# Sink attention and a soft mixture of experts on one core: the cast of q and k between the exponentials, in the rounds around a sequence's first block

## The chip, the cores and the metric

The kernel runs on one core of a Trainium2 chip, as one program. The metric is the time of one execution on the device in microseconds; lower is better. The core's engines are TensorE (PE in the profile, its weight loads PEld), VectorE (DVE), ScalarE (ACT), GpSimd (POOL) and SyncE (SP), which here only issues transfers. Each works through its own list of instructions in order and waits on semaphores for the others.

## The reference: what is computed

Attention over 4 sequences of 768 tokens with 8 heads of 64, where a token sees the first 4 tokens (the sinks) and the last 128; then a mixture of 8 experts whose weights come from 8 rounds of normalising rows and columns. Cut to what matters:

```python
scores = scale * np.matmul(q, k.transpose(0, 1, 3, 2))
keep = is_sink | in_window            # first 4 keys, or the last 128
scores = np.where(keep, scores, -1000000000.0)
a = np.exp(scores - np.max(scores, axis=-1, keepdims=True))
a = a / (np.sum(a, axis=-1, keepdims=True) + 1e-09)
attn = np.matmul(a, v)                # 4 x 8 x 768 x 64
x = attn.transpose(0, 2, 1, 3).reshape(3072, 512)
P = np.exp(x @ w_gate - max)          # 3072 x 8, then 8 rounds of P /= row sums, P /= column sums
for e in range(8):
    out += P[:, e:e + 1] * (np.maximum(x @ w1[e], 0.0) @ w2[e])
```

All is fp32. The kernel multiplies fp32 numbers as two parts, a rounded high part and the low part that is left; most operands are split by a cast on ScalarE (high) and a subtraction on VectorE (low), and a product is three matmuls.

## The kernel before, in words

The attention comes first and takes some 290 us; the matmuls of the experts fill the rest and, a few at a time, the gaps of the attention. The tokens are worked in 48 units: unit n is (sequence b, block i of 128 tokens, half hh of four heads), so a sequence has 12 units and its first block (i = 0) is units 0 and 1, 12 and 13, 24 and 25, 36 and 37. A token block attends to itself and the block before it; the first block has nothing before it and no separate sinks, so for its units TensorE has three matmuls with V for two heads, where others have six and one with the sinks.

The units run as a software pipeline. Round n (`steady_round`, from n = 10 on) does the scores, the maxima and the exponentials of unit n + 1, transposes q and k of unit n + 2, transposes the probabilities of unit n and multiplies those of unit n - 1 with V. Within a round the engines' orders are written out by hand: what the code calls first stands first on its engine, and no scheduler changes it. The steps, with the lines of the profile:

- `scores` (L484): TensorE, 12 matmuls of 128x260 for four heads, each head into a PSUM bank of its own, st0 to st3. There is one buffer of each, so a bank must have been read before it is written again.
- `soften` (L492, L495): for each head VectorE adds the mask and takes the row's extreme (L492), then ScalarE takes the exponential with its row sum (L495). The four heads go one after the other.
- `values` for the first pair of heads (L558) and six matmuls of an expert's first layer (`run_fill`, L660) on TensorE. Every second time these complete a sum, ScalarE applies the relu (L665) and VectorE makes its low part (L666), which waits in the list `late`.
- `transpose_qk` (L446, L450, L453, L456): TensorE transposes q and k of the unit after the next into st0, ScalarE casts the high part into the tile `KQ` (L450), and a function that it returns has VectorE subtract the low part (L453) and, where i = 1, copy the sink columns (L456). That function is put into the list `lows`. The next round's scores read the result.
- `divide` (L501, L502, L504): VectorE adds 1e-9 to the four row sums and inverts them, GpSimd scales the probabilities of the four heads. L501 needs the sums of all four exponentials.
- `late`, then `lows`: the relu's low part, then that of q and k.
- `transpose_p` twice (L515, L517, L520): TensorE transposes the probabilities of two heads into st1, then of the other two into st2; ScalarE casts the high part PT (L517), VectorE subtracts the low part (L520). In a first block these tiles are 256 wide, else 512.
- `values` for the second pair, `store_x` (L568, copies of the result on ScalarE and VectorE), the transposed sinks (L538, L540), and a second portion of expert matmuls (L676).

GpSimd's list in a round is the gathered sinks (L532, L533), the split of V (L464, L465) and the scaling (L504); in the rounds of a first block also the sinks of the new sequence spread over the heads (L419) and split (L425, L426), and in some rounds the low part of the finished tokens (L577).

So ScalarE's order in a round is: four exponentials, the relu if there is one, the cast of q and k, two casts of probabilities, the copy of the result. VectorE's is: four extremes, the row sums and their inverse, the relu's low part, the low part of q and k, two low parts of probabilities, the copy. The code that sets it:

```python
        if on(n + 1):
            for h in range(HH):
                soften(n + 1, (h,))
...
        lows = [transpose_qk(n + 2)] if on(n + 2) else []
        flush(mid)
        behind[0] = True
        if on(n + 1):
            divide(n + 1, range(HH))
        flush(late)
        flush(lows)
```

Of the kernel before, what the change touches and what calls it, by code (L numbers as in the profile page):

```python
# [229 lines left out]
def tile_sink_attention_moe(ctx: ExitStack, tc: tile.TileContext, q, k, v, wg, w1, w2, out):  # L230
# [17 lines left out]
    HH = H // 2  # L248
# [59 lines left out]
    def split_gate():  # L308
        for kc in range(KC):
            nc.vector.tensor_copy(wgr[:, kc, :], zero)  # L310
        nc.vector.tensor_copy(wgr[:, :, 0:E], wg_raw)
        nc.vector.tensor_sub(wgr[:, :, E:2 * E], wg_raw, f32(wgr[:, :, 0:E]))
        nc.vector.tensor_add(sel, ident[0:2 * E, 0:E], ident[0:2 * E, E:2 * E])
# [82 lines left out]
    units = [(b, i, hh) for b in range(B) for i in range(NB) for hh in range(2)]  # L396
    us = {}
# [8 lines left out]
    def flush(todo):  # L406
        for f in todo[:]:
            f()
        todo.clear()

    def load_sinks(b):
        vs = VSr[b] = att.tile([SK, D], F32, name="vs")
        for r0 in range(0, SK, NK):
            (nc.sync if b else nc.scalar).dma_start(vs[r0:r0 + NK, :], v[b, :, 0:SINK, :])
# [13 lines left out]
    def load_rows(names, j):  # L428
        b, i = divmod(j, NB)
        cuts = (0, HH, H) if j == 0 else (0, H)  # L430
        ts = [(att.tile([P, H, D], F32, name=nm), {"kr": k, "qr": q, "vr": v}[nm]) for nm in names]
        for (t, _), nm in zip(ts, names):
            raws[nm, b, i] = t
        for h0, h1 in zip(cuts, cuts[1:]):
            for t, src in ts:
                nc.sync.dma_start(t[:, h0:h1, :], src[b, h0:h1, i * P:(i + 1) * P, :].rearrange("h p d -> p h d"))
# [47 lines left out]
                nc.tensor.matmul(ps[h], lhsT=Q[r0:r0 + D, a, pr, :], rhs=K[r0:r0 + D, c, pr, :],  # L484
                                 start=(j == 0), stop=(j == 2))

    def soften(n, hs):

        b, i, hh = units[n]
        sc, st, ps = (us[n][x] for x in ("sc", "st", "ps"))  # L490
        for h in hs:
            nc.vector.tensor_tensor_reduce(out=sc[:, h, :], in0=ps[h], in1=masks[place(b, i).start, min(i, 2)], op0=ALU.add, op1=ALU.min,  # L492
                                           scale=-scale, scalar=3.0e38, accum_out=st[:, 0, h:h + 1])
        for h in hs:
            nc.scalar.activation(sc[:, h, :], sc[:, h, :], AF.Exp, bias=st[:, 0, h:h + 1], scale=-1.0, accum_out=st[:, 1, h:h + 1])  # L495

# [116 lines left out]
    def gate_step():  # L613
        if gates and next(gates[0], 0) == 0:
            gates.pop(0)
            gate_step()
# [104 lines left out]
    def run_fill(k_):  # L721
        for _ in range(k_):
            next(fill, None)
# [43 lines left out]
    on = lambda j: 0 <= j < L  # L767

    def early_round(n):

        if units[n + 2][2] == 0:
            with (tc.high_priority() if n == -2 else nullcontext()):
                load_rows(("kr", "qr"), n // 2 + 1)
                load_rows(("vr",), n // 2 + 1)
            if units[n + 2][1] == 0:
                load_sinks(units[n + 2][0])
        if n == -2:
            nc.sync.dma_start(wg_raw, wg.rearrange("(k p) e -> p k e", p=P))
        if n == 2:
            with tc.issue_after(us[1]["split"][1]):  # L780
                split_gate()
        if on(n + 1):
            for pr in range(NP):
                scores(n + 1, pr)
                soften(n + 1, range(2 * pr, 2 * pr + 2))
                divide(n + 1, range(2 * pr, 2 * pr + 2))
        if on(n - 1):
            values(n - 1, 0)
        if n >= START:
            run_fill(1)  # L790
        gate_step()
        for j in (0, 1) if n == -2 else (n + 2,) if n >= 0 else ():
            transpose_qk(j)()
        if on(n):
            transpose_p(n, 0)()
            with (tc.issue_after(us[n - 1]["scaled"]) if n > 1 else nullcontext()):
                split_v(n)
        gate_step()
        if on(n):
            transpose_p(n, 1)()  # L800
        if on(n - 1):
            values(n - 1, 1)
            store_x(n - 1)
        gate_step()
        if on(n) and units[n][1]:
            gather_sinks(n)
            transpose_sinks(n)
        if on(n) and units[n][1:] == (0, 1):
            with tc.issue_after(us[n]["scaled"]):
                spread_sinks(units[n][0])  # L810
                split_sinks(units[n][0])
        if n >= START:
            run_fill(1)
# [3 lines left out]

    def steady_round(n):

        if n % 2 == 0:  # L820
            if on(n + 2):
                load_rows(("vr",), n // 2 + 1)
            for j in (n // 2 + 1, n // 2 + 2) if n == STEADY else (n // 2 + 2,):
                if on(2 * j):
                    load_rows(("kr", "qr"), j)
            if on(n + 2) and units[n + 2][1] == 0:
                load_sinks(units[n + 2][0])
        if n in ROWS:
            ROWS[n][0](ROWS[n][1])
        mid.extend(coming)  # L830
        coming.clear()
        behind[0] = False
        if on(n + 1):
            for pr in range(NP):
                scores(n + 1, pr)
        if on(n):
            if units[n][1]:
                gather_sinks(n)
            split_v(n)
        if on(n + 1):  # L840
            for h in range(HH):
                soften(n + 1, (h,))
        if on(n - 1):
            values(n - 1, 0)
        run_fill(1)
        gate_step()
        lows = [transpose_qk(n + 2)] if on(n + 2) else []
        flush(mid)
        behind[0] = True
        if on(n + 1):  # L850
            divide(n + 1, range(HH))
        flush(late)
        flush(lows)
        if on(n):
            lows.append(transpose_p(n, 0))
        gate_step()
        if on(n):
            lows.append(transpose_p(n, 1))
        flush(lows)
        if on(n - 1):  # L860
            values(n - 1, 1)
            store_x(n - 1)
        gate_step()
        if on(n) and units[n][1]:
            transpose_sinks(n)
        run_fill(1)
        if n in PIECES:
            in_turn(*plain_tiles(*PIECES[n]))
        if n == L - 8:
            first_pieces.extend(pieces1(0))  # L870
        if n in (L - 8, L - 6, L - 4, L - 3):
            in_turn(*first_pieces.pop(0))
        flush(act_end)
        if on(n):
            b, i, hh = units[n]
            if (i, hh) == (0, 0):
                spread_sinks(b)
            elif (i, hh) == (0, 1):
                split_sinks(b)
        flush(pool_end)  # L880
        if L - 10 <= n < L - 6:
            sums1(0, n - (L - 10))
# [327 lines left out]
    hs = {}  # L1210
# [450 lines left out]
```

## Time and profile before

| what | value |
|---|---|
| time, median of 3 runs | 2137.17 us (2137.05 to 2137.85) |
| the profiled execution | 2136.98 us, of which the span from the first to the last instruction is 2135.3 us |
| TensorE busy | 2118.8 us, 99% of the span |
| VectorE, ScalarE, GpSimd busy | 1525.7, 883.9 and 749.6 us |
| granted TensorE clock | 1.000 throughout |
| rounds 12 to 14, 24 to 26, 36 to 38 start (first score matmul) | 82.18, 154.22 and 224.16 us |

A row of a timeline reads: start in us, duration in us, engine, line, operation, the tile written and those read, shapes, how many in a row, and in brackets how long the engine had been idle and which instruction ended that. A row of the list of waits reads: who waited for whom, us in total, how often, the longest. A duration goes to the end of the writing, so the next instruction of the same engine may start some 0.1 us before it.

### The profile page before, as it was taken

The numbers are of one execution on the slowest core, as the hardware profiler recorded it, in microseconds if no ns is written. First come the engines' busy times: TensorE is split into PE (matmuls) and PEld (weight loads), VectorE is DVE, ScalarE is ACT, GpSimd is POOL, SyncE is SP. The second block draws the span as 40 slices with busy tenths as digits, with TensorE's granted clock in tenths as the row PEclk, the third lists the DMA queues.
The fourth block names the chain that finished last, engine by engine and source line by source line (L and its number), as shares of the span: only waits on it lengthen the run. The fifth ranks groups of instructions, "written<-read, shape, count | busy, mean of one in ns | idle before, by whom it ended". The sixth has DMA issues, their size and how long they took to land.

```text
span 2135.3 us, 31724 instructions
## 1 busy us (share of the span) xinstructions
PE 2118.8 (99%) x10501; PEld 1770.3 (83%) x10501; DVE 1525.7 (71%) x2747; ACT 883.9 (41%) x1867; POOL 749.6 (35%) x950
## 2 busy tenths in 40 slices
PE   8999999999999999999999999999999999999998
PEld 7898897888888888888888888888888888888887
DVE  8777778877777876766666666666657666676666
ACT  7777745444444444442333223332333223332232
POOL 7756643333232331232223322233323222232223
PEclk9999999999999999999999999999999999999999
DMA  6534427999999987686666666667866666666662
GB/s 144 127 84 100 95 80 244 312 307 315 289 315 292 307 290 251 213 283 202 204 194 200 207 193 201 207 198 262 298 203 196 199 207 194 201 207 189 206 197 86
DMA packets 397641, 453.82 MB, mean 213 GB/s; under 512 B 99680, under 2 KB 265760, under 8 KB 396576
## 3 DMA queue, kind: packets, MB, share of 16 engines
q1 hardware_dynamic: 397080, 451.57, 68.0%
q8 instruction: 86, 1.41, 0.3%
q14 instruction: 83, 0.68, 0.1%
q10 hardware_dynamic: 392, 0.16, 0.0%
HBM read 314.17 MB, written 137.46 MB: 212 GB/s over the span
## 4 chain that ended last, share of the span: by engine, by line
PE 94%; DVE 3%; ACT 2%; issue 0%; POOL 0%; DMA 0%; SPq 0%; DVEq 0%; ACTq 0%; POOLq 0%
PE c L926 41%; PE o L1485 20%; PE held L1485 8%; PE held L1170 7%; PE o L1170 7%; PE O L558 3%; PE st L484 2%; PE st L515 1%; PE o L676 1%; PE g L660 1%; ACT sc L495 1%; PE st L446 1%; PE st L660 0%; DVE PT L520 0%; DVE KQ L453 0%; DVE sc L492 0%
## 5 line engine op out<-in xcount | busy, mean ns | idle before, releaser
L952 ACT CAST hf<-w 128x512 fp32r<-128x512 f32 x448 | 265.5, 622 | 562.3 <-POOL w L1452 299.8
L1485 PE MATMUL o<-hf,W2q 128*128 128x512 f32 x1920 | 472.0, 389 | 0.0
L1485 PEld LDWEIGHTS o<-hf,W2q 128*128 128x128 f32 x1920 | 360.0, 188 | 75.4 <-DVE acc L1499 0.9
L926 PE MATMUL c<-T,W1q 128*128 128x512 f32 x1530 | 388.8, 389 | 0.2 <-DVE w L1433 0.2
L953 DVE TENSOR_TENSOR hf<-w,hf 128x512 fp32r<-128x512 f32 x448 | 330.4, 765 | 74.8 <-ACT hf L952 67.0
L926 PEld LDWEIGHTS c<-T,W1q 128*128 128x128 f32 x1530 | 286.8, 188 | 60.7 <-DVE w L1433 0.9
L1499 DVE TENSOR_TENSOR acc<-o,acc 128x512 f32<-128x512 f32 x298 | 204.7, 687 | 171.2 <-PE o L1485 171.2
L926 PE MATMUL c<-B,W1q 128*128 128x512 f32 x1134 | 278.3, 389 | 0.0
L1452 POOL TENSOR_TENSOR w<-w 128x512 f32<-128x512 f32 x64 | 82.8, 1293 | 492.4 <-DVE w L1434 492.4
L926 PEld LDWEIGHTS c<-B,W1q 128*128 128x128 f32 x1134 | 212.6, 188 | 44.0
L1433 DVE TENSOR_TENSOR w<-c,M 128x512 f32<-128x512 f32 x192 | 132.2, 689 | 138.2 <-PE c L926 132.9
L1429 ACT COPY M<-c 128x512 f32<-128x512 f32 x192 | 112.7, 587 | 248.9 <-PE c L926 248.8
L1485 PE MATMUL held<-hf,W2q 128*128 128x512 f32 x768 | 194.8, 389 | 0.0
L926 PE MATMUL c<-T,W1f 128*128 128x512 f32 x672 | 171.1, 390 | 0.1
L1170 PE MATMUL held<-W2f,h 128*128 128x512 f32 x672 | 171.1, 390 | 0.0
L1170 PE MATMUL o<-W2f,h 128*128 128x512 f32 x672 | 170.6, 389 | 0.1
L1485 PEld LDWEIGHTS held<-hf,W2q 128*128 128x128 f32 x768 | 144.0, 188 | 29.8
L1467 POOL TENSOR_TENSOR w<-w 128x512 f32<-128x512 f32 x64 | 105.7, 1652 | 176.0 <-DVE hf L953 176.0
L1170 PEld LDWEIGHTS o<-W2f,h 128*128 128x128 f32 x672 | 126.0, 188 | 27.0 <-DVE acc L1177 0.9
L926 PEld LDWEIGHTS c<-T,W1f 128*128 128x128 f32 x672 | 125.8, 188 | 26.9 <-issue 0.5
L1170 PEld LDWEIGHTS held<-W2f,h 128*128 128x128 f32 x672 | 125.9, 188 | 26.4 <-DVE W2f L953 0.5
L979 POOL TENSOR_TENSOR r<-r 128x256 f32<-128x256 f32 x27 | 20.1, 743 | 359.3 <-ACT M L1133 222.9
(224 smaller groups left out, 3086.7 us busy)
## 6 DMA issues: line engine op xcount, KB each, us to landing
W2q<-w2s SPq DMA_DIRECT2D x448, 256.0 KB, 3.1
W1q<-w1s SPq DMA_DIRECT2D x444, 256.0 KB, 2.9
w1s<-W1f SPq DMA_DIRECT2D x56, 896.0 KB, 7.5
w2s<-WT SPq DMA_DIRECT2D x136, 256.0 KB, 3.6
r<-in_moe_w_dram SPq DMA_DIRECT2D x64, 512.0 KB, 4.6
w2s<-W2f SPq DMA_DIRECT2D x56, 256.0 KB, 4.8
PB<-psd SPq DMA_DIRECT2D x16, 512.0 KB, 3.8
w2s<-W2f SPq DMA_DIRECT2D x56, 128.0 KB, 6.5
```

Source lines behind the costliest of these rows:

```text
L484: nc.tensor.matmul(ps[h], lhsT=Q[r0:r0 + D, a, pr, :], rhs=K[r0:r0 + D, c, pr, :], start=(j == 0), stop=(j == 2))
L558: nc.tensor.matmul(u["O"][:, pr], lhsT=x_, rhs=y_, start=(j == 0), stop=(j == len(ops) - 1))
L926: nc.tensor.matmul(ps, lhsT=w1(a, k), rhs=x[:, b, k, :], start=(start and j == 0), stop=(stop and j == len(TERMS) - 1), skip_group_check=n ...
L952: nc.scalar.copy(dst[:, 0], src)
L953: at(1, lambda: nc.vector.tensor_sub(dst[:, 1], src, f32(dst[:, 0])))
L1170: nc.tensor.matmul(o, lhsT=h[c, th][:, a, off:off + P], rhs=W2F[n][:, w, c, :], start=(begin and c == 0 and j == 0), stop=(end and c == 1 ...
L1429: nc.scalar.copy(t, T["c2"])
L1433: nc.vector.tensor_add(w, T["c1"], T[m])
L1452: nc.gpsimd.tensor_sub(S3, T["A11"], T["A21"])
L1467: at(k, lambda: nc.gpsimd.tensor_sub(T["A11"], w, T["A11"]))
L1485: nc.tensor.matmul(o, lhsT=W2Q[part, n, m][:, a, k * P:(k + 1) * P], rhs=F[part, n, H_OF[m]][:, w, :], start=(j == 0 and (begin or not hol ...
L1499: nc.vector.tensor_add(sums[m, k], o, sums[m, k])
```

## The change

`soften` is cut in two, `maxima` (VectorE's part) and `exponentials` (ScalarE's). In a round of which unit n or unit n - 1 is of a first block (`short`; from the tenth round on these are rounds 12, 13, 14, 24, 25, 26, 36, 37 and 38) only two exponentials stand ahead of the transposes of q and k. The cast of q and k follows on ScalarE, its low part on VectorE is made at once, then the other two exponentials come, and the row sums after them. In all other rounds, and in the first ten, each engine's order is as before.

```diff
-    def soften(n, hs):
+    def maxima(n, hs):
...
+    def exponentials(n, hs):
+
+        sc, st = us[n]["sc"], us[n]["st"]
         for h in hs:
             nc.scalar.activation(sc[:, h, :], sc[:, h, :], AF.Exp, bias=st[:, 0, h:h + 1], scale=-1.0, accum_out=st[:, 1, h:h + 1])
...
     def steady_round(n):
 
+        short = on(n + 2) and 0 in (units[n][1], units[n - 1][1])
...
         if on(n + 1):
-            for h in range(HH):
-                soften(n + 1, (h,))
+            maxima(n + 1, range(HH))
+            exponentials(n + 1, range(2 if short else HH))
...
         lows = [transpose_qk(n + 2)] if on(n + 2) else []
         flush(mid)
         behind[0] = True
+        if short:
+            flush(lows)
+            exponentials(n + 1, range(2, HH))
         if on(n + 1):
             divide(n + 1, range(HH))
         flush(late)
         flush(lows)
```

From the exponential on, lines stand four further on in the changed kernel (the exponential is L499 there, the sums L505 and L506, the low part of the probabilities L524), and behind `steady_round` nine further on.

ScalarE in round 24, before. The names: sc the scores, h the expert's hidden tile, KQ the split q and k, st a PSUM bank, PT the probabilities, xr the result.

```order
L495 ACTIVATE sc,st<-sc,st 128x260 x4
L665 ACTIVATE h_2388<-g_2595 128x256
L450 CAST KQ_174<-st_2704 128x2x2x128
L517 CAST PT<-st_2720 128x256
L517 CAST PT<-st_2725 128x256
L568 COPY xr<-O 64x256
```

And in the changed kernel:

```order
L499 ACTIVATE sc,st<-sc,st 128x260 x2
L669 ACTIVATE h_2388<-g_2595 128x256
L450 CAST KQ_174<-st_2702 128x2x2x128
L499 ACTIVATE sc,st<-sc,st 128x260 x2
L521 CAST PT<-st_2720 128x256
L521 CAST PT<-st_2725 128x256
L572 COPY xr<-O 64x256
```

The third and fourth exponential have moved behind the relu and the cast of q and k.

VectorE in the same round, before, from the end of the extremes (L492) on. L589 is a gate column of the experts, copied out of PSUM.

```order
L492 ISA sc,st<-st_2670,mask_79 128x260
L492 ISA st 128x1
L589 COPY Xt<-O 128x8
L501 TENSOR_SCALAR st<-st 128x4
L502 RECIPROCAL st<-st 128x4
L666 SCALAR_TENSOR_TENSOR h_2388<-g_2595,h_2388 128x256
L453 TENSOR_TENSOR KQ_174<-st_2704,KQ_174 128x2x2x128
L456 CAST KQ_174<-KQ_174 128x4x4
L520 TENSOR_TENSOR PT<-st_2720,PT 128x256
L520 TENSOR_TENSOR PT<-st_2725,PT 128x256
```

And in the changed kernel:

```order
L492 ISA sc,st<-st_2670,mask_79 128x260
L492 ISA st 128x1
L593 COPY Xt<-O 128x8
L453 TENSOR_TENSOR KQ_174<-st_2702,KQ_174 128x2x2x128
L456 CAST KQ_174<-KQ_174 128x4x4
L505 TENSOR_SCALAR st<-st 128x4
L506 RECIPROCAL st<-st 128x4
L670 SCALAR_TENSOR_TENSOR h_2388<-g_2595,h_2388 128x256
L524 TENSOR_TENSOR PT<-st_2720,PT 128x256
L524 TENSOR_TENSOR PT<-st_2725,PT 128x256
```

The low part of q and k, with the sink columns, has moved ahead of the row sums; the low parts of the probabilities stay last. TensorE's, GpSimd's and SyncE's lists are the same.

More of the change, by code (lines that the diff above doesn't have):

```diff
@@ L784, in early_round @@
                 scores(n + 1, pr)
-                soften(n + 1, range(2 * pr, 2 * pr + 2))
+                maxima(n + 1, range(2 * pr, 2 * pr + 2))
+                exponentials(n + 1, range(2 * pr, 2 * pr + 2))
                 divide(n + 1, range(2 * pr, 2 * pr + 2))
```

## The prediction

> **What bounds the kernel now.** I read the page first, for the engine that sets the span.
>
> ```profile
> span 2135.3 us, 31724 instructions
> ...
> PE 2118.8 (99%) x10501; PEld 1770.3 (83%) x10501; DVE 1525.7 (71%) x2747; ACT 883.9 (41%) x1867; POOL 749.6 (35%) x950
> ```
>
> TensorE is busy for all but 16.5 us of 2135.3, and its order is fixed by hand, so whatever makes it wait in the attention part is carried to the end, and a wait taken away there is gained. The profiled execution took 2136.98 us, 1.7 more than its span and 0.19 less than the median of 2137.17; I work from 2136.98. Next I asked for TensorE's waits from 76 to 246 us, the stretch that holds all nine rounds that the change touches (12 to 14, 24 to 26, 36 to 38):
>
> ```profile
> PE st L484 <- DVE KQ L456: 1.0, 1, 1.0
> PE st L484 <- DVE PT L520: 0.6, 3, 0.2
> ```
>
> Only the scores (L484) wait, 1.6 us in all: once for the low part of k and q (L453, with the copy of the sink columns L456 behind it), three times for the low part of the probabilities (L520), whose PSUM banks the next round's scores overwrite. So two VectorE steps compete to end last. The change brings one forward, and the question is what it does to the other. The timeline of rounds 24 and 25 shows the chain. ScalarE:
>
> ```profile
> 156.97 0.50 ACT L495 ACTIVATE sc<-sc,st 128x260 f32<-128x260 f32 x1
> ...
> 157.46 0.36 ACT L665 ACTIVATE h<-g 128x256 fp32r<-128x256 f32 x1
> 157.72 0.57 ACT L450 CAST KQ<-st 128x512 fp32r<-128x512 f32 x1
> 158.19 0.37 ACT L517 CAST PT<-st 128x256 fp32r<-128x256 f32 x1
> ```
>
> The first row is the fourth exponential; the next ones start 0.5, 0.26 and 0.47 us after each other. VectorE, in the same round:
>
> ```profile
> 157.59 0.17 DVE L501 TENSOR_SCALAR st<-st 128x4 f32<-128x4 f32 x1 [0.29 <-ACT sc L495]
> 157.79 0.18 DVE L502 RECIPROCAL st<-st 128x4 f32<-128x4 f32 x1
> 157.88 0.40 DVE L666 SCALAR_TENSOR_TENSOR h<-g,h 128x256 fp32r<-128x256 f32 x1
> 158.33 0.69 DVE L453 TENSOR_TENSOR KQ<-st,KQ 128x512 fp32r<-128x512 f32 x1
> 158.93 0.18 DVE L456 CAST KQ<-KQ 128x16 fp32r<-128x16 f32 x1
> 159.02 0.74 DVE L520 TENSOR_TENSOR PT<-st,PT 128x256 fp32r<-128x256 f32 x2
> ```
>
> VectorE waits for the fourth exponential (L501 starts 0.62 after it), then works without a gap to L520. TensorE, rounds 24 to 26 (the first, third and fifth row are the last transpose of q and k of a round, the others the first product with V after the scores of the next):
>
> ```profile
> 157.30 0.27 PE L446 MATMUL st<-ident,qr 128*128 128x128 f32 x1
> ...
> 160.40 0.62 PE L558 MATMUL O<-PT,V 128*128 128x256 f32 x3
> ...
> 162.08 0.27 PE L446 MATMUL st<-ident,qr 128*128 128x128 f32 x1
> ...
> 165.38 0.62 PE L558 MATMUL O<-PT,V 128*128 128x256 f32 x3
> ...
> 167.04 0.27 PE L446 MATMUL st<-ident,qr 128*128 128x128 f32 x1
> ```
>
> ```profile
> 170.06 1.23 PE L484 MATMUL st<-KQ 64*128 64x260 f32 x11 [0.21 <-DVE PT L520]
> 171.22 0.98 PE L558 MATMUL O<-PT,V 128*128 128x256 f32 x6
> ```
>
> And VectorE's sums and low parts of rounds 25 and 26:
>
> ```profile
> 162.85 0.17 DVE L501 TENSOR_SCALAR st<-st 128x4 f32<-128x4 f32 x1 [1.12 <-ACT sc L495]
> ...
> 164.00 0.75 DVE L520 TENSOR_TENSOR PT<-st,PT 128x256 fp32r<-128x256 f32 x2
> ...
> 167.84 0.45 DVE L501 TENSOR_SCALAR st<-st 128x4 f32<-128x4 f32 x1 [0.81 <-ACT sc L495]
> ...
> 169.32 1.28 DVE L520 TENSOR_TENSOR PT<-st,PT 128x512 fp32r<-128x512 f32 x2
> ```
>
> TensorE's first product comes 1.38 us after L520 starts (159.02 to 160.40, 164.00 to 165.38), and 1.90 after it where the low parts are twice as wide (169.32 to 171.22). So the start of L520 is the clock that TensorE follows in these rounds.
>
> **The change part by part.** No instruction is added or removed; names and line numbers below are those of the kernel before.
>
> The exponentials. The cast L450 now stands between the second and the third, so these two wait until TensorE has transposed q and k. The transposes end 0.27 after their last start; I put the cast 0.04 behind that, as L453 starts 0.04 after the cast's end above (157.72 + 0.57 = 158.29, and 158.33). In round 24 the cast then starts at 157.30 + 0.27 + 0.04 = 157.61, which is only 0.11 before the 157.72 of now. The two exponentials that are left follow 0.47 later and 0.50 apart, and L501 0.62 behind the last: 157.30 + 1.90 = 159.20, where it is 157.59 now. So the sums come 1.61 later to buy 0.11 for the cast. The relu L665 stays ahead of the cast, and its matmuls ahead of the transposes, so it does not end last.
>
> The low part. L453 and L456 run in VectorE's wait, from 158.2 to 159.0. Behind L501 the path to L520 is then shorter: 0.20 and 0.09 to L666 and 0.30 more (0.40 less the 0.1 by which L520 overlaps L456), 0.60 in all with a relu's low part, 0.30 without. L520 starts at 159.20 + 0.60 = 159.80, **0.78 later** than the 159.02 of now. ScalarE's cast of the probabilities, 0.50 behind the fourth exponential, is out by 159.4 and hides.
>
> Round 25 starts 0.78 late. L501: 162.08 + 0.78 + 1.90 = 164.76; no relu here, so L520 at 165.06, **1.06 late** in all. Round 26: L501 at 167.04 + 1.06 + 1.90 = 170.00. Its length is 0.17 or 0.45 in the rows above; the long one ran until GpSimd's L464 was out (167.84 + 0.45 = 168.29 against 167.85 + 0.41):
>
> ```profile
> 163.41 1.87 POOL L504 TENSOR_SCALAR sc<-sc,st 128x260 f32<-128x260 f32 x4 [1.20 <-ACT KQ L450]
> ...
> 167.85 0.41 POOL L464 TENSOR_SCALAR V<-vr 128x256 fp32r<-128x256 f32 x1
> ```
>
> L504 follows L501 by 0.56, so it moves to 165.32, and L464, 4.44 behind it, ends at 170.17: L501 takes 0.19. Then 0.04 + 0.09 + 0.30 to L520 at 170.62, **1.30 late** (1.28 with 0.17, 1.56 with 0.45). The third sequence has the same rows 69.9 us later,
>
> ```profile
> 228.96 0.74 DVE L520 TENSOR_TENSOR PT<-st,PT 128x256 fp32r<-128x256 f32 x2
> ...
> 239.25 1.28 DVE L520 TENSOR_TENSOR PT<-st,PT 128x512 fp32r<-128x512 f32 x2
> ```
>
> so it costs 1.30 too. The first one, rounds 12 to 14, has the long wait for the low part. TensorE, VectorE and GpSimd:
>
> ```profile
> 85.09 0.27 PE L446 MATMUL st<-ident,qr 128*128 128x128 f32 x1
> ...
> 89.87 0.27 PE L446 MATMUL st<-ident,qr 128*128 128x128 f32 x1
> ...
> 92.63 1.21 PE L484 MATMUL st<-KQ 64*128 64x260 f32 x12 [0.99 <-DVE KQ L456]
> ...
> 95.28 0.27 PE L446 MATMUL st<-ident,qr 128*128 128x128 f32 x1
> ```
>
> ```profile
> 86.98 0.74 DVE L520 TENSOR_TENSOR PT<-st,PT 128x256 fp32r<-128x256 f32 x2
> ...
> 91.13 0.46 DVE L501 TENSOR_SCALAR st<-st 128x4 f32<-128x4 f32 x1 [1.43 <-ACT sc L495]
> ...
> 92.39 0.74 DVE L520 TENSOR_TENSOR PT<-st,PT 128x256 fp32r<-128x256 f32 x2
> ...
> 97.57 1.28 DVE L520 TENSOR_TENSOR PT<-st,PT 128x512 fp32r<-128x512 f32 x2
> ...
> 101.94 0.68 DVE L501 TENSOR_SCALAR st<-st 128x4 f32<-128x4 f32 x1 [1.12 <-ACT sc L495]
> ```
>
> ```profile
> 86.11 1.86 POOL L504 TENSOR_SCALAR sc<-sc,st 128x260 f32<-128x260 f32 x4 [2.34 <-DVE st L502]
> ...
> 90.83 0.74 POOL L465 TENSOR_TENSOR V<-vr,V 128x256 fp32r<-128x256 f32 x1
> ```
>
> Round 12: L501 at 85.09 + 1.90 = 86.99, L520 at 87.59, 0.61 late. Round 13: L501 at 89.87 + 0.61 + 1.90 = 92.38. GpSimd's L504 is at 86.99 + 0.56 = 87.55 and L465, 4.72 behind, runs 92.27 to 93.01, so L501 ends at 93.03 and L520 starts 0.13 later, at 93.16: 0.77 late, or 0.29 if L501 takes 0.17. Here the 0.99 of TensorE goes (the low part is done by 92.3), but L520 starts its wait anew. Round 14: L501 at 97.95, with 0.32 by the same reckoning of GpSimd's queue, L520 at 98.70, 1.13 late (0.50 with short L501s throughout). The next round's L501, 0.68 long now, finds GpSimd at another place and gives back some 0.1: 1.0 for this sequence, between 0.5 and 1.1.
>
> On this one step a rule bears. The Trainium skill, page "SBUF — State Buffer", section "SBUF: two separate sides", says that VectorE and GpSimd share a port pair that the first comer holds for its whole instruction while the other is blocked. The rows agree (0.17 alone, 0.45 until L464 is out); were the 0.46 of round 13 a fixed length instead, the first sequence would cost about 0.8 and the sum would be 3.4.
>
> The sum: 1.0 + 1.3 + 1.3 = **3.6 us**, from 3.1 (0.5 + 2 x 1.28) to 4.25 (1.13 + 2 x 1.56). 2136.98 + 3.6 = **2140.6**. The rounds behind have no recorded wait of TensorE that could take the delay in. SyncE's order and GpSimd's are unchanged, so loads and stores only shift with the buffers.
>
> **The rivals.** A measurement of this kernel can tell about 0.2%, 4.3 us, from no change: 2132.9 and 2141.4 are the bounds.
>
> Not slower: the low part of q and k decides, and L520 comes no later. For it speaks the largest wait, 1.0 for L456. It decides if the sums are delayed by less than VectorE's path to L520 is shortened; against it, in round 24 they are 1.61 against 0.84 (159.02 less 157.88 + 0.30), in round 25 1.13 of its own against 0.85, and for the balance to turn the transposes would have to end half a microsecond sooner. It would save at most the 1.6 of the waits: 2135.4. Chance 0.08.
>
> No net change: TensorE does not follow L520 but has slack there, since in round 24 no wait of the scores is recorded. Against it, the 1.38 is the same where it is recorded to wait. Slack of 1.3 in each sequence gives 2137.0. Chance 0.08.
>
> Worse: GpSimd becomes the bound. Its L504 of round 25 moves by 1.91 (163.41 to 165.32) while TensorE is only 1.06 late, so the scaled probabilities and sink columns come 0.85 nearer to their readers on TensorE. If these have less slack than that, each sequence loses up to 0.85 more: 3.6 + 2.6 gives 2143.2. Against it, no wait of TensorE for GpSimd stands in the list above. Chance 0.14.
>
> **How the numbers follow.** Forecast 0.70, with a range of its own of 2140.0 to 2141.3; the others as given. The range from 2136.9 to 2142.3 takes in the case without change and the smaller half of the worse one, and leaves out the gain and the rest of the worse one, some 0.17. Faster by over 0.2%: no case reaches it, 0.02. Slower by over 0.2%: most of the worse case and the tail of the forecast, 0.17. Within: 0.81.
>
> **What would show it.** In the changed kernel's timeline of the nine rounds the cast L450 should start right behind the last transpose, L501 1.90 us behind that transpose's start, and L520 0.6 (0.3 in the middle round) later; TensorE's waits for L456 should be gone and those for L520 grown to 3 us or more, with the spans from L520 to L558 still 1.38 and 1.90. From 250 us on all should lie 3.6 later. I am wrong if L520 moves less than half a microsecond in round 24, if TensorE's products no longer follow it, or if TensorE waits for GpSimd.

## The result, and the profile after

The changed kernel takes 2141.26 us (median, 2140.42 to 2142.02) where the kernel before takes 2137.36 beside it: a ratio of 1.0018 with a 95% interval of 1.0011 to 1.0025, 3.9 us slower. Forecast were 2140.6 and 3.6 us. The profiled execution took 2141.48 us, 1.7 more than its span; the page of the changed kernel:

```profile
span 2139.8 us, 31724 instructions
...
PE 2118.6 (99%) x10501; PEld 1768.9 (83%) x10501; DVE 1524.5 (71%) x2747; ACT 885.1 (41%) x1867; POOL 749.7 (35%) x950
```

The engines' busy times have moved by 1.4 us at most, the span by 4.5: the added time is waiting, not work. TensorE's waits from 76 to 250 us say for what:

```profile
PE st L484 <- DVE PT L524: 3.2, 9, 0.9
PE st L542 <- POOL SS L537: 0.9, 3, 0.4
```

Line numbers are now those of the changed kernel: the exponential is L499, the sums L505, the low part of the probabilities L524, the products with V L562. The wait for the low part of q and k is gone, that for the probabilities comes in nine places instead of three and makes 3.2 us, where 3 or more were forecast, and one has appeared that the prediction did not have in its sum, for the sinks that GpSimd gathers (L537). The prediction had named a wait for GpSimd as one of its signs of being wrong; what it is worth is asked below. ScalarE in round 24, from the relu on, shows the new order:

```profile
158.19 0.38 ACT L669 ACTIVATE h<-g 128x256 fp32r<-128x256 f32 x1 [0.44 <-PE g L664]
158.80 0.59 ACT L450 CAST KQ<-st 128x512 fp32r<-128x512 f32 x1 [0.23 <-PE st L446]
159.28 0.52 ACT L499 ACTIVATE sc<-sc,st 128x260 f32<-128x260 f32 x1
...
159.79 0.50 ACT L499 ACTIVATE sc<-sc,st 128x260 f32<-128x260 f32 x1
...
160.29 0.62 ACT L521 CAST PT<-st 128x256 fp32r<-128x256 f32 x2
```

ScalarE now stands idle twice, for the expert's matmuls (0.44) and for the transposes (0.23), with two exponentials queued behind. VectorE in the same round:

```profile
159.42 0.69 DVE L453 TENSOR_TENSOR KQ<-st,KQ 128x512 fp32r<-128x512 f32 x1 [0.94 <-ACT KQ L450]
160.03 0.17 DVE L456 CAST KQ<-KQ 128x16 fp32r<-128x16 f32 x1
160.42 0.17 DVE L505 TENSOR_SCALAR st<-st 128x4 f32<-128x4 f32 x1 [0.23 <-ACT sc L499]
...
160.72 0.39 DVE L670 SCALAR_TENSOR_TENSOR h<-g,h 128x256 fp32r<-128x256 f32 x1
161.03 0.74 DVE L524 TENSOR_TENSOR PT<-st,PT 128x256 fp32r<-128x256 f32 x2
```

Even with the low part of q and k ahead of them the sums wait 0.23 for the fourth exponential: in this round it is ScalarE that ends last. The round starts at 155.41 (before: 154.22), 1.19 later, so the sums are 160.42 - 157.59 - 1.19 = 1.64 late and L524 is 161.03 - 159.02 - 1.19 = 0.82 late. TensorE in the three rounds of this sequence, from the last transpose of round 24 on:

```profile
158.49 0.27 PE L446 MATMUL st<-ident,qr 128*128 128x128 f32 x1
...
160.67 0.38 PE L484 MATMUL st<-KQ 64*128 64x260 f32 x1
161.50 0.99 PE L484 MATMUL st<-KQ 64*128 64x260 f32 x11 [0.45 <-DVE PT L524]
162.41 0.62 PE L562 MATMUL O<-PT,V 128*128 128x256 f32 x3
...
166.77 0.99 PE L484 MATMUL st<-KQ 64*128 64x260 f32 x11 [0.20 <-DVE PT L524]
167.69 0.62 PE L562 MATMUL O<-PT,V 128*128 128x256 f32 x3
...
171.09 0.32 PE L542 MATMUL st<-ident,SS 128*96 128x128 f32 x1 [0.24 <-POOL SS L537]
...
172.62 1.23 PE L484 MATMUL st<-KQ 64*128 64x260 f32 x11 [0.20 <-DVE PT L524]
173.77 0.98 PE L562 MATMUL O<-PT,V 128*128 128x256 f32 x6
```

The list of waits shows only part of the delay. Before, the twelve score matmuls of round 25 run without a break:

```profile
159.48 0.99 PE L484 MATMUL st<-KQ 64*128 64x260 f32 x12
```

Now the first starts alone at 160.67 and the other eleven 0.83 later. Of these 0.83 us the list has 0.45; the rest is the lone matmul's row of 0.38, which counts as busy. So the listed waits grow by 2.5 us (4.1 against 1.6) where the stretch defined next grows by 3.7.

I measure all runs by one stretch of TensorE's timeline: from round 12's first score matmul to the first product with V of round 39. Before it takes 241.14 - 82.18 = 158.96 us, after 245.07 - 82.39 = 162.68, which is 3.72 longer: 0.98 in the first sequence (round 12 to round 24, 155.41 - 82.39 against 154.22 - 82.18), 1.36 in the second (to round 36, at 226.71 and 224.16) and 1.38 in the third. The rest of the 4.5 us by which this one span is longer lies ahead of the stretch (0.2) and behind it (0.6); the medians differ by 3.9.

### The profile page after: what moved, and what is told of

It reads as the page before. It is cut to its first block, busy times and chain, and to the rows that moved or that the text cites. A ratio compares the mean times of both kernels' runs of the same rounds, so it can differ in the third digit from the quotient of the medians.

```text
span 2139.8 us, 31724 instructions
## 1 busy us (share of the span) xinstructions
PE 2118.6 (99%) x10501; PEld 1768.9 (83%) x10501; DVE 1524.5 (71%) x2747; ACT 885.1 (41%) x1867; POOL 749.7 (35%) x950
## 4 chain that ended last, share of the span: by engine, by line
PE 96%; DVE 2%; ACT 1%; issue 0%; DMA 0%; SPq 0%; ACTq 0%; DVEq 0%
PE c L935 41%; PE o L1494 20%; PE held L1494 8%; PE held L1179 7%; PE o L1179 7%; PE O L562 3%; PE st L484 2%; PE g L664 2%; PE st L519 2%; PE o L680 1%; PE st L446 1%; ACT sc L499 1%; PE st L664 0%; PE O L680 0%; PE O L590 0%; DVE PT L524 0%
```

## The experiments

Each line number in this section is the changed kernel's. "The stretch" is the one just described, 158.96 us before and 162.68 after. Each ratio is to the kernel before on the same chip, which took 2137.0 to 2137.5 us.

**One half alone: ScalarE's order.** The cast stands between the exponentials, but VectorE makes the low part of q and k where it did before, behind the sums.

```diff
         if short:
-            flush(lows)
             exponentials(n + 1, range(2, HH))
```

> Only ScalarE's half of the change: the cast of q and k stands between the second and third exponential in the nine rounds, VectorE keeps its old order (row sums, relu's low part, then the low part of q and k). Stretch meant here and below: from the first score matmul of round 12 to the first product with V of round 39, 158.96 us before and 162.68 in the changed kernel (3.72 more). Theory (the exponentials wait behind the transposes, so sums and the low part of the probabilities come late): the low part of q and k is no longer hidden in VectorE's wait and comes on top, 0.6 to 0.7 a round, so some 10 us over before, 9 to 11: time near 2147, 0.45% over before. Rival (VectorE's new order is what costs): no dearer than before, 2137 to 2138.

Measured: 2151.52 us, ratio 1.0069 (1.0055 to 1.0083), stretch 170.53, 11.57 longer than before. TensorE's waits from 76 to 262 us:

```profile
PE st L484 <- DVE KQ L456: 7.4, 6, 1.4
PE st L484 <- DVE KQ L453: 2.3, 2, 1.2
PE st L484 <- ACT B L580: 1.3, 1, 1.3
PE st L484 <- DVE PT L524: 0.3, 2, 0.2
```

The third line names ScalarE's copy L580, which ended at 101.09; the low part of q and k that these scores read had ended at 101.00, so it is most likely the same wait as in the first two lines. The direction and the place are as expected, the size is more. The sequences cost 2.80, 5.16 and 3.61; the second has something of its own, which shows in the granted clock (the 0.85 and 0.72 behind the five engines' busy times):

```profile
172.00:176.00 4.00, 3.19 (x26) 2.71 (x24) 1.87 (x9) 3.77 (x14) 3.39 (x8) 1.00 0.01 2
176.00:180.00 4.00, 3.51 (x24) 3.01 (x25) 3.30 (x12) 1.80 (x8) 3.03 (x8) 0.85 0.20 66
180.00:184.00 4.00, 4.00 (x30) 4.00 (x29) 1.88 (x5) 2.27 (x6) 2.81 (x8) 0.72 0.61 140
```

In these 8 us TensorE loses 4 x 0.15 + 4 x 0.28 = 1.7 us to its clock. Without them the stretch is 9.9 longer, inside the 9 to 11. The same happens again behind the third sequence (0.89 from 247 to 262 us), which is most of the 2.0 us that this execution's span has gained behind the stretch. So moving the cast alone costs about 1.1 us a round on average: 1.5 to 1.7 in a first round, some 1.0 in the others, and 0.4 in round 13, which had the long wait already. The second half of the change takes most of this back, from 11.57 to 3.72.

**The other half alone: VectorE's order.** All four exponentials ahead of the cast, the low part of q and k ahead of the sums.

```diff
-            exponentials(n + 1, range(2 if short else HH))
+            exponentials(n + 1, range(HH))
...
         if short:
             flush(lows)
-            exponentials(n + 1, range(2, HH))
```

> Only VectorE's half: four exponentials first and the cast behind the relu as before, but the low part of q and k ahead of the row sums. Theory: the cast still comes when it came before, so the sums now wait for the low part instead: the low part of the probabilities 0.6 late in a first round, 0.3 more in the second, 0.4 more in the third; stretch 3 to 4.5 us over before, time near 2141. Rival (the wait of the exponentials behind the transposes is not what costs, the moved low part is): the same 3.7 or so here, but then the run with ScalarE's half alone is not dearer than before; only both together tell.

Measured: 2141.43 us, ratio 1.002 (1.0011 to 1.0029), stretch 162.84, 3.88 longer than before and within 0.2 of the whole change. As expected: it costs the same because here the sums wait for the low part (round 24: L505 starts at 159.48, right behind L456) instead of for the fourth exponential. Either half delays the sums, and the whole change is no worse than its second half.

**One exponential behind the cast instead of two.**

```diff
-            exponentials(n + 1, range(2 if short else HH))
+            exponentials(n + 1, range(3 if short else HH))
...
             flush(lows)
-            exponentials(n + 1, range(2, HH))
+            exponentials(n + 1, range(3, HH))
```

> As the changed kernel, but the cast and the low part of q and k stand behind the third exponential instead of the second. Theory: only one exponential waits, and the transposes are out nearer to its turn: low part of the probabilities 0.3 late in a first round, 0.2 early in a second, about even in a third. Stretch within 0.5 us of before (from -0.8 to +0.5), time near 2137. Rival (any cast between exponentials, or the low part ahead of the sums, costs by itself): at least half of the 3.7 stays, 2139 or more.

Measured: 2139.24 us, ratio 1.0009 (0.9999 to 1.0018), stretch 161.01. It was to come back to about the kernel before; 2.05 of the 3.72 remained, so the expectation missed, and the rival's figure (half or more, 2139 or more) came out. ScalarE and VectorE in round 24 of this kernel:

```profile
158.87 0.59 ACT L450 CAST KQ<-st 128x512 fp32r<-128x512 f32 x1 [0.23 <-PE st L446]
159.35 0.52 ACT L499 ACTIVATE sc<-sc,st 128x260 f32<-128x260 f32 x1
159.49 0.69 DVE L453 TENSOR_TENSOR KQ<-st,KQ 128x512 fp32r<-128x512 f32 x1 [0.94 <-ACT KQ L450]
...
160.10 0.17 DVE L456 CAST KQ<-KQ 128x16 fp32r<-128x16 f32 x1
160.18 0.16 DVE L505 TENSOR_SCALAR st<-st 128x4 f32<-128x4 f32 x1
```

The last exponential would have released the sums at 159.35 + 0.62 = 159.97; the low part holds VectorE to 160.18. I had counted the path of ScalarE alone. The sums start at the later of two times, the last exponential's start plus 0.62 and the cast's start plus 1.31 (158.87 to 160.18). In the change itself the first is the later by 0.3, as the prediction had it when it put the low part of q and k into VectorE's wait.

**The change with early transposes.** The changed kernel, with the transposes of q and k, the cast and the last two exponentials ahead of the expert's six matmuls and their relu in these rounds. The prediction had put the point from which the change turns at transposes that end half a microsecond sooner.

```diff
+        lows = [transpose_qk(n + 2)] if short else []
+        if short:
+            flush(lows)
+            exponentials(n + 1, range(2, HH))
         run_fill(1)
         gate_step()
-        lows = [transpose_qk(n + 2)] if on(n + 2) else []
+        if on(n + 2) and not short:
+            lows = [transpose_qk(n + 2)]
         flush(mid)
         behind[0] = True
-        if short:
-            flush(lows)
-            exponentials(n + 1, range(2, HH))
```

> As the changed kernel, but in the nine rounds TensorE transposes q and k ahead of the expert's six matmuls (and the relu that these feed stands behind the fourth exponential), so the cast finds its input when the second exponential is out. Theory (it is the wait for the transposes that costs): the sums come only 0.5 to 0.7 late and VectorE's path is 0.6 to 0.85 shorter, so the low part of the probabilities comes 0.1 early in a first round, 0.4 to 0.5 more in the second, 0.2 to 0.4 more in the third; stretch 1 to 2.6 us below before, time near 2135. Rivals: the split of the exponentials costs by itself, or GpSimd's later scaling decides: still 1 us or more over before.

Measured: 2135.28 us, ratio 0.9992 (0.9983 to 1.0001), stretch 156.97, 1.99 shorter than before. TensorE's waits in the stretch:

```profile
PE st L542 <- POOL SS L537: 0.9, 3, 0.6
PE st L484 <- DVE PT L524: 0.3, 1, 0.3
```

In round 24 the last transpose starts 2.19 us into the round (155.27 less 153.08) where it was 3.08 (158.49 less 155.41), 0.89 sooner; L524 starts 4.73 into the round, against 4.80 before and 5.62 with the change alone. The sign turns as forecast. The gain in time is at the edge of what the comparison can tell, that in the stretch is plain.

**The control: early transposes alone**, in the kernel before's order of ScalarE and VectorE (`turn_qk` is the transposes of `transpose_qk` by themselves; the cast and all else stays in its old place).

```diff
-            exponentials(n + 1, range(2 if short else HH))
+            exponentials(n + 1, range(HH))
...
+        lows = []
+        if short:
+            turn_qk(n + 2)
         run_fill(1)
         gate_step()
-        lows = [transpose_qk(n + 2)] if on(n + 2) else []
+        if on(n + 2):
+            lows = [transpose_qk(n + 2)]
         flush(mid)
         behind[0] = True
-        if short:
-            flush(lows)
-            exponentials(n + 1, range(2, HH))
```

> The kernel before, but with TensorE's transposes of q and k ahead of the expert's six matmuls in the nine rounds; ScalarE's and VectorE's orders are as before. Theory: the cast waits for the four exponentials and the relu, not for the transposes, so nothing moves: stretch within 0.4 us of the 158.96 of before, time near 2137. Rival to the theory of the run with early transposes and split exponentials (its gain comes from the transposes alone): 1 us or more below before.

Measured: 2137.21 us, ratio 1.0 (0.9991 to 1.0009), stretch 159.06, 0.10 longer than before. Early transposes bring nothing while the cast waits behind four exponentials, and the cast's new place costs 3.7 while the transposes are late. Together they save 2.0.

**By rounds: first rounds alone, and middle rounds alone.** The new order only in rounds 12, 24 and 36, and in a second kernel only in 13, 25 and 37.

```diff
-        short = on(n + 2) and 0 in (units[n][1], units[n - 1][1])
+        short = on(n + 2) and units[n][1:] == (0, 0)
```

```diff
-        short = on(n + 2) and 0 in (units[n][1], units[n - 1][1])
+        short = on(n + 2) and units[n][1:] == (0, 1)
```

> The change in rounds 12, 24 and 36 alone (the first round of each sequence start). Theory, by the prediction's terms: 0.6 + 0.8 + 0.8, so the stretch is 2.0 to 2.4 us over before and the time near 2139.5. Rival (the low part of q and k is the bound and the loss lies in the third rounds, where GpSimd is late): under 1 us.

> The change in rounds 13, 25 and 37 alone. Theory: 0.28 each in rounds 25 and 37; in round 13 the long wait for the low part of q and k goes and GpSimd's queue stands where it stood, so the sums are not held and the low part of the probabilities comes 0.3 early: stretch from -0.1 to +0.5 over before, time near 2137.5. Rival (each of the nine rounds costs the same 0.4): 1.2 us over before.

Measured: first rounds 2139.03 us, ratio 1.0009 (1.0 to 1.0018), stretch 160.82, 1.86 longer than before; middle rounds 2136.99 us, ratio 1.0 (0.9991 to 1.0009), stretch 158.76, 0.20 shorter. Both lie a little below what was expected. With the first rounds alone the one long wait for the low part of q and k, round 13's, is still there:

```profile
PE st L484 <- DVE PT L524: 1.8, 5, 0.4
PE st L484 <- DVE KQ L456: 1.0, 1, 1.0
```

With the middle rounds alone it is gone, and the first sequence is 0.49 us shorter for it (71.55 against 72.04), while the second is 0.15 longer (22.36 against 22.21 from round 24 to round 28). So the part of the change that meets the wait it removes does gain; it is one round of nine. The 2.1 that are left by difference (3.72 - 1.86 + 0.20) are not the third rounds' own, for an unchanged round behind a changed one gives part of the delay back: with first rounds alone TensorE is 0.83 late behind round 24 and 0.68 behind round 26, with middle rounds alone 0.28 behind round 25 and 0.13 behind round 26.

In the changed kernel itself, counted from a sequence's first score matmul to the first product with V behind each of its three rounds, TensorE is 0.65, 0.76 and 1.14 late in the first sequence, 0.82, 1.12 and 1.36 in the second, 0.83, 1.11 and 1.38 in the third. So the first rounds add 2.3, the middle ones 0.7, the third ones 0.9, and 0.2 comes back behind round 14. No run had the third rounds alone.

**Is the new wait for GpSimd part of the loss?** GpSimd's split of the sinks (L425, L426, at 168.40 to 170.38 in round 26 and in the way of the gathered sinks) moved behind the split of V in the third round.

```diff
             split_v(n)
+            if units[n][1:] == (1, 0):
+                split_sinks(units[n][0])
...
-            elif (i, hh) == (0, 1):
-                split_sinks(b)
```

> The changed kernel, but GpSimd splits the new sequence's sinks (two instructions, 1.9 us) in the third round behind the split of V instead of at the end of the second, so that the gathered sinks are ready sooner; its scaling comes when it came. The changed kernel's trace has TensorE wait for those gathered sinks three times, 0.9 us in all. Theory: that wait is hidden in the wait for the low part of the probabilities behind it, so the wait list loses it and the stretch stays within 0.25 us of the changed kernel's 162.68. Rival (GpSimd is part of the loss): the stretch is 0.7 to 0.9 us shorter.

Measured: 2146.01 us, ratio 1.0038 (1.0024 to 1.0052), stretch 168.03, 5.35 longer than the changed kernel. The wait for the sinks is gone, but neither theory had this time. GpSimd, VectorE and TensorE in round 14:

```profile
96.99 1.26 POOL L426 TENSOR_TENSOR VS<-vm,VS 32x512 fp32r<-32x512 f32 x1
...
97.15 1.14 DVE L505 TENSOR_SCALAR st<-st 128x4 f32<-128x4 f32 x1 [0.31 <-ACT sc L499]
...
98.72 1.28 DVE L524 TENSOR_TENSOR PT<-st,PT 128x512 fp32r<-128x512 f32 x2
...
99.46 1.23 PE L484 MATMUL st<-KQ 64*128 64x260 f32 x11 [1.62 <-DVE PT L524]
```

The sums, 0.17 us long in most rounds, lasted until GpSimd's L426 ended (96.99 + 1.26 = 98.25), and TensorE waited 1.62. And after that wait its clock fell to half for 3 us:

```profile
98.00:101.00 3.00, 1.54 (x13) 1.22 (x14) 2.90 (x9) 1.24 (x6) 2.56 (x6) 0.96 0.14 50
101.00:104.00 3.00, 3.00 (x16) 3.00 (x16) 1.77 (x8) 2.05 (x8) 2.59 (x7) 0.50 0.79 255
104.00:107.00 3.00, 3.00 (x24) 2.59 (x24) 1.90 (x4) 2.09 (x5) 2.79 (x8) 0.97 0.77 174
```

That is 1.7 us; from 172 to 180 us the same happens again (0.98 and 0.59, another 1.7). 5.35 less 3.4 leaves some 0.65 for each sequence, near the 0.8 by which the sums last longer (1.14, 0.94 and 0.95 against 0.33, 0.17 and 0.17). Whether the wait for the sinks counts can't be read from this run.

**The same question without the long hold:** the sinks split behind the gathered sinks and ahead of the split of V, so that the sums meet the short L464 as they do now.

```diff
             if units[n][1]:
                 gather_sinks(n)
+            if units[n][1:] == (1, 0):
+                split_sinks(units[n][0])
             split_v(n)
...
-            elif (i, hh) == (0, 1):
-                split_sinks(b)
```

> The changed kernel, with one thing moved on GpSimd in the third round of each sequence (14, 26, 38): the sinks are split (L425, L426) ahead of the split of V instead of behind the gathered sinks' own place at the end, so that the transposed sinks (L542) of TensorE should find them ready. Theory (TensorE follows the low part of the probabilities, and the new wait of 0.9 us for the sinks only uses up time in which TensorE would stand before the scores anyway): the wait for GpSimd goes from the list, that for the low part grows by as much, and the stretch from round 12's first score matmul to round 39's first product with V stays within 0.25 of the changed kernel's 162.68 us. Rival (GpSimd has become a bound and its 0.9 us is part of the loss): the stretch is 0.7 to 0.9 us shorter, 161.8 to 162.0. What could blur it: if VectorE's sums (L505) of these rounds meet a longer GpSimd instruction than the 0.41 us one of now, they are held by up to 0.8 us and each sequence loses as much.

Measured: 2140.97 us, ratio 1.0017 (1.0008 to 1.0026), stretch 162.71 against 162.68. All of TensorE's waits in the stretch:

```profile
PE st L484 <- DVE PT L524: 4.8, 9, 0.9
```

The wait for the sinks is gone, that for the probabilities has grown by more than its 0.9, and the stretch is the same: GpSimd's wait was hidden in front of the other, as the theory had it. The sums of rounds 26 and 38 last 0.1 longer here than in the changed kernel, too little to hide a gain of 0.7.

**The same in the change with early transposes**, where the other wait is nearly gone and GpSimd's should count. The edit is the one just shown, on top of the early transposes.

> The kernel with the transposes of q and k and the last two exponentials ahead of the expert's matmuls (which measured 2135.28 us and a stretch of 156.97 us), with GpSimd's split of the sinks moved forward as in the run beside it. There TensorE waited 0.9 us for the sinks in three places and only 0.3 us for the probabilities' low part, so the wait for GpSimd is no longer behind another. Theory: it counts now, and without it the stretch is 0.4 to 0.9 us shorter, 156.1 to 156.6 us, the time near 2134.7 us. Rival: another wait takes its place (the low part of the probabilities), and the stretch stays at 157.0 us within 0.25.

Measured: 2135.81 us, ratio 0.9993 (0.9984 to 1.0002), stretch 157.36, 0.39 longer than the change with early transposes. The theory missed, and so did the rival's 157.0 within 0.25. VectorE's sums in round 14 of this kernel, where L426 ran from 95.61 to 96.90:

```profile
96.29 0.63 DVE L505 TENSOR_SCALAR st<-st 128x4 f32<-128x4 f32 x1 [0.30 <-ACT sc L499]
```

Again the sums were held to the end of L426, so this run could not answer either. For the last two, the sinks' work went into the 3.1 us or more in which GpSimd stands idle in a sequence's first round: all of it (L419, L425, L426) in one kernel, all but L426 in the other, which there stands at that round's end.

```diff
             split_v(n)
+            if units[n][1:] == (0, 0):
+                spread_sinks(units[n][0])
+                split_sinks(units[n][0])
...
-            b, i, hh = units[n]
-            if (i, hh) == (0, 0):
-                spread_sinks(b)
-            elif (i, hh) == (0, 1):
-                split_sinks(b)
```

```diff
             split_v(n)
+            if units[n][1:] == (0, 0):
+                spread_sinks(units[n][0])
+                high_sinks(units[n][0])
...
             b, i, hh = units[n]
             if (i, hh) == (0, 0):
-                spread_sinks(b)
-            elif (i, hh) == (0, 1):
-                split_sinks(b)
+                low_sinks(b)
```

> The kernel with early transposes (2135.28 us, stretch 156.97 us, 0.9 us of waits for the sinks left), now with GpSimd's three instructions that spread and split the sinks (L419, L425, L426: 1.05 + 0.62 + 1.28 = 2.95 us) moved into the 3.1 us in which GpSimd stands idle in the first round of a sequence, behind its split of V. Theory (in that kernel the wait for the sinks counts, and the run that moved the sinks' split within the third round lost it again only because VectorE's sums met the 1.28 us instruction there): no wait for the sinks, and the sums of the second and third round meet at most the 0.4 us instruction of V; against that the sums of the first round may be held by up to 0.4 us by the end of L426. Stretch 156.1 to 156.8 us, time near 2134.9. Rival (the low part of the probabilities ends within a tenth of the sinks' wait in any case): stretch 156.9 to 157.2.

> As the run beside it, but only the spreading and the high part of the sinks (1.05 + 0.62 = 1.67 us) go into GpSimd's idle time of the first round, and the low part (1.28 us) stands at that round's end where the spreading stood, so that no long GpSimd instruction lies where the first round's sums start. GpSimd's work in the second round then begins 0.2 us later than with early transposes alone, which may hold the sums there by up to 0.8 us (they start 0.03 us ahead of the low part of V there). Theory: no wait for the sinks; first round as with early transposes alone; stretch 156.1 to 156.8 us if the second round's sums are held by no more than 0.2, up to 2 us longer if they meet the low part of V in each sequence. Rival: 156.9 to 157.2 without any such hold.

Measured: 2135.67 us, ratio 0.9994 (0.9985 to 1.0003), stretch 157.41; and 2135.53 us, ratio 0.9991 (0.9982 to 1.0), stretch 157.08. The wait for the sinks is gone in both and nothing is gained. In the first of the two the later sequences are as in the change with early transposes to 0.01 us (21.64 against 21.63 from round 24 to round 28, and 12.30 against 12.31 from round 36's sums to the end of the stretch), so the rival's reason holds: the probabilities end as late in any case. The second run is inside the rival's range too. The 0.44 by which the first run's stretch is longer, and which puts it outside both ranges, come from round 12, GpSimd and VectorE:

```profile
85.61 0.69 DVE L453 TENSOR_TENSOR KQ<-st,KQ 128x512 fp32r<-128x512 f32 x1 [0.85 <-ACT KQ L450]
...
85.84 1.28 POOL L426 TENSOR_TENSOR VS<-vm,VS 32x512 fp32r<-32x512 f32 x1
...
86.22 0.94 DVE L456 CAST KQ<-KQ 128x16 fp32r<-128x16 f32 x1
```

The copy of the sink columns, 0.17 long in most rounds, lasted until L426 ended. Of the versions tried, the change with early transposes has the shortest stretch; the three that build on it are 0.1 to 0.45 us longer there. Their times can't be told apart (ratios 0.9991 to 0.9994, each to within 0.0009).

## Why the prediction was right, point by point

**What bounds the kernel.** That TensorE follows the start of the probabilities' low part held in all three kinds of round: from L524 to the first product 1.38, 1.37 and 1.89 us (161.03 to 162.41, 166.32 to 167.69, 171.88 to 173.77), forecast 1.38, 1.38 and 1.90. The case without change, which needed slack there, falls with it. What TensorE's list of waits had kept out of sight there is the lone score matmul shown above.

**The sums' delay.** The step "L501 starts 1.90 behind the last transpose" measured 1.93, 1.92 and 1.92 in rounds 24 to 26. The difference is the exponential behind the cast, which takes 0.52 instead of 0.50 in the rows above and lets the next one start 0.51 later. Over three rounds that is 0.07, and it is why the second and third sequence cost 1.36 and 1.38 where 1.30 was forecast.

**The path behind the sums.** From L505 to L524 0.61 and 0.61 in the rounds with a relu, 0.30 in the middle one (166.02 to 166.32), as taken.

**The first sequence, with GpSimd's hold.** Forecast were late starts of the low part by 0.61, 0.77 and 1.13 and 0.1 given back, 1.0 in all. Measured, less the 0.21 us by which round 12 starts later in this execution, the three are 0.65, 0.78 and 1.14, and the sequence cost 0.98. The term that could have gone wrong is round 13, where the sums' length was taken from GpSimd's queue:

```profile
92.50 0.72 POOL L465 TENSOR_TENSOR V<-vr,V 128x256 fp32r<-128x256 f32 x1
...
92.66 0.59 DVE L505 TENSOR_SCALAR st<-st 128x4 f32<-128x4 f32 x1 [0.21 <-ACT sc L499]
...
93.38 0.72 DVE L524 TENSOR_TENSOR PT<-st,PT 128x256 fp32r<-128x256 f32 x2
```

They run until L465 is out (93.22), and 93.38 less the 0.21 by which this execution is later is 93.17, forecast 93.16. The other reading, a fixed 0.46, is ruled out by the 0.59 here and by the 1.14 and 0.94 of the experiments. The Trainium skill, page "SBUF — State Buffer", section "SBUF: two separate sides", has the shared port pair held for a whole instruction; these rows agree.

**The sum.** 0.98 + 1.36 + 1.38 = 3.72 in the stretch against 3.6, 3.9 by the medians. The agreement holds term by term, so it is not luck. That the kernel stays within 0.2% of before is a near thing: 1.0018, with an interval that reaches 1.0025.

**Not slower.** It needed transposes half a microsecond sooner. With 0.89 sooner the same order of ScalarE and VectorE is 1.99 us faster in the stretch than before; with early transposes and the old order nothing happens. The condition was the right one in kind; half a microsecond itself was not run, and in round 24 the 0.89 sooner made the low part of the probabilities only 0.07 earlier than before. The case's ceiling, at most the 1.6 us of the listed waits, was too low: 1.99 were saved, and the list leaves a part of the waiting out. The case had also left out that VectorE's low part can itself end behind the exponentials, as it does with one exponential behind the cast.

**Worse, by GpSimd.** This rival was right in its mechanism and wrong in its price. It had the scaling of round 25 move by 1.91; measured are 1.98 (163.41 to 166.58, less the 1.19 by which the sequence starts later). The split of the sinks and the gathering of the sink columns follow on GpSimd without a gap and move with it. Before, the gathered sinks were out half a microsecond ahead of TensorE's transpose of them in round 26:

```profile
167.66 0.23 POOL L533 TENSOR_TENSOR SS<-sc,SS 128x16 fp32r<-128x16 f32 x1
...
168.38 0.27 PE L538 MATMUL st<-ident,SS 128*96 128x128 f32 x1
```

In the changed kernel they come just ahead of the transpose at 171.09, which waits 0.24:

```profile
170.81 0.22 POOL L537 TENSOR_TENSOR SS<-sc,SS 128x16 fp32r<-128x16 f32 x1
```

So TensorE does wait for GpSimd, 0.9 us in three places, for the sink columns and not for the scaled probabilities. It costs nothing, since the stretch is the same without it (162.71 and 162.68). The sign of being wrong that the prediction had named came true without its being wrong.

**What stays open.** The 0.6 us that this one profiled execution loses behind the stretch have no recorded wait that the kernel before lacks, and no run was made for them. They don't go with the delay: behind the stretch every other profile is 0.3 to 2.1 us longer than before's, the control with the stretch of before by 0.3 and the change with early transposes, whose stretch is shorter, by 0.8.

## What to carry to other kernels

On an engine that works in order, a step moved ahead of others hands them its own wait, not its length: here a cast that came 0.11 us sooner made the row sums 1.6 us later. Before moving it, compare two numbers in each round, how much later the steps behind it start and how much shorter their way to the bound becomes (1.61 against 0.84); the move pays only if what the step waits for is brought forward first, and then both together gave what neither gave alone. The list of waits of the bounding engine is not a list of prices: here 2.5 us more of listed waits went with 3.7 us of time, and a listed wait of 0.9 was worth nothing. A wait isn't a loss until a run without it is shorter.

## What the hardware showed unexpectedly

Two tiny VectorE steps between SBUF tiles last until a GpSimd instruction that runs beside them ends: the sums of 128x4, 0.17 us alone, took 0.59, 0.63 and 1.14, and the copy of 128x16, 0.17 alone, took 0.94. The subtraction that reads PSUM is not held: L453 took its 0.69 at 85.61 with L426 running from 85.84 to 87.12, and before, from 60 to 290 us, all 38 of them took 0.66 to 0.69, though GpSimd was already at work when 30 of them started. So it matters which GpSimd instruction stands where such a step starts, more than how much GpSimd has to do.

A wait of TensorE can cost more than its length. In the run with 1.62 us of waiting at 99.46 the granted clock was 0.50 from 101 to 104 us, and 0.59 from 176 to 180 behind a wait of 1.42; with the waits of up to 1.4 of ScalarE's half alone it fell to 0.72 in the second sequence and below 0.9 behind the third. Each time some 1.7 us were lost on top. In the other twelve profiles, whose waits are 1.0 us or less, the clock in the stretch is 1.00 throughout. The Trainium skill, page "TensorE: Matmul & The Clock Gate", section "Part 1: The HAM clock gate (the "warmup" mystery)", has the clock halved after an idle window of about 3.4 us; here waits of less than half of that were enough, in a stretch of 3 us in which TensorE was busy for 1.54. Not every such wait did it (the first sequence of ScalarE's half alone kept its full clock), and what decides was not tried.
